# Summing V in four column tiles of the tensor engine, with per-pair sums on the vector engine, in a decode attention kernel

## The chip, the cores and the metric

One core of a Trainium2 chip. The metric is device time in microseconds (us) of one execution; lower is better. Engine names: PE is the tensor engine (PEld its weight loads), DVE the vector engine, ACT the scalar engine, POOL GpSimd, SP the engine that issues the input transfers.

## The reference

A gate mixes two branches; nearly all bytes and work are in branch A, a one-token attention over a cache.

```python
B, Sq, D = 4, 1, 1024
H, Sk, Dh = 32, 8192, 128          # k_cache, v_cache: (4, 32, 8192, 128) bf16 each
q = (x @ wq).reshape(B, Sq, H, Dh).transpose(0, 2, 1, 3)
scores = einsum("bhqd,bhkd->bhqk", q, k_cache) * Dh ** -0.5
p = softmax(scores)
o = einsum("bhqk,bhkd->bhqd", p, v_cache)
a = o.transpose(0, 2, 1, 3).reshape(B, Sq, H * Dh) @ wo
# branch B: a gated MLP, 1024 -> 3584 -> 1024, on the same four rows
# out = g * a + (1 - g) * b,  g = sigmoid(sum(x * gate_w))
```

K and V together are 537 MB, each read once. Everything else is 39 MB.

## The kernel before

The 128 heads are taken four at a time (a "pair" in the kernel's words is a K or a V load of four heads, 8 MB), 32 pairs of each. Four pairs form a group, which shares one softmax. SP loads into a ring of five 4 MB slots; a load waits until the slots are free. In the steady state the order is K pair d, then V pair d-4, and so on; the last four V pairs come alone, and then the output weights `wo`.

```python
# K pair (cut): DVE transposes a stretch, PE multiplies it
for n in range(RD):                                   # RD = 8 stretches
    flat_t = turned(P, CJ * P)                        # one of three transpose buffers
    nc.vector.transpose(out=flat_t.bitcast(U32), in_=kn[...])
    ... 8 matmuls 128x128 by 128x512 into S_ps ...

# V pair (cut): weights are the spread probabilities PB, 32 columns wide
row = NM * t                                          # NM = 32; t = pair in the group
for c in range(RD):
    for z in range(2):
        for w in range(2):
            for e in range(2):
                j0 = CJ * (c % JT) + 16 * z + 8 * w + 4 * e
                nc.tensor.matmul(o_ps[row:row + NM, e, :],
                                 lhsT=PB[:, RD * t + c, z, w]...,
                                 rhs=vn[:, j0 * Dh:(j0 + 4) * Dh],
                                 start=(n == 0), stop=(n == 4 * RD - 1))
if t < GD - 1:
    return
# once per group (cut): take from o_ps the half that is wanted, then select by matmul
nc.scalar.activation(out=o_sb[:], in_=o_ps[:, 0, :], func=ACT.Copy, scale=mE[:, 0:1])
nc.vector.scalar_tensor_tensor(out=o_sb[:], in0=o_ps[:, 1, :], scalar=mE[:, 1:2], in1=o_sb[:], ...)
... four fp32 matmuls with selg give oT ...

# output block (cut): eight matmuls with 4 rows, two column halves in turn
for r in range(r0, r1):
    for n in range(NH):
        mm_acc(acc[:, n * NB:(n + 1) * NB], LT[:, r, g, :], w[:, r, n * NB:(n + 1) * NB])
```

All 64 matmuls of one V pair write the same 32 rows of `o_ps`, that is, the same column tile of the array. At the end, behind the last V pair, the order on PE is: the last eight V matmuls, output block, selection, output block, a small turn of the new rows (`o_rows`), and 32 more output matmuls.

## Time and profile before

| | before |
|---|---|
| time | 1343.79 us median of 4 |
| bytes in | 576 MB at 429 GB/s |
| PE busy, DVE busy | 1032.8 us (77%), 614.4 us (46%) |
| one V pair on PE at full clock | 13.9 us |
| last V piece landed; last matmul ended | 1323.8 us; 1339.4 us |

These are lines of the page of the kernel before: busy time of each engine, then the span in 40 equal slices (busy tenths of PE; the granted clock of PE in tenths; the share of time in which the DMA engines were busy; what they moved).

```profile
PE 1032.8 (77%) x4552; PEld 227.9 (17%) x2364; DVE 614.4 (46%) x369; ACT 50.6 (4%) x46; POOL 62.8 (5%) x161
...
PE   2565878787788687778977779597778679877898
...
PEclk9787988888998888889988889888889899888899
DMA  9999999999999999999999999999999999999997
GB/s 414 436 432 431 439 434 427 445 430 422 445 424 430 442 432 426 438 434 428 438 436 426 432 430 434 436 433 438 428 423 436 430 431 442 436 419 444 419 425 325
```

The DMA row is full until the last slice. No engine is: the kernel is bound by the rate at which its bytes come in.

The costliest groups of instructions of the kernel before (line, engine, operation, output and inputs, shapes, count; then busy us and mean ns of one; then the idle time in front and what ended most of it). The view keeps different shapes apart.

```profile
L436 DVE STREAM_TRANSPOSE TB<-ring 128x2048 uint32<-128x2048 uint32 x256 | 566.9, 2277 | 492.4 <-DMA ring<-in_A_k_cache_dram 491.5 <-PE S_ps L442 0.8
L442 PE MATMUL S_ps<-TB,Z 128*128 128x512 bf16 x2048 | 518.8, 408 | 219.4 <-DVE TB L436 218.9
L513 PE MATMUL o_ps<-ring,PB 128*32 128x512 bf16 x2048 | 461.4, 388 | 52.6 <-DMA ring<-in_A_v_cache_dram 48.1 <-ACT PB L484 4.6
...
L457 DVE TENSOR_REDUCE mx<-S_ps 128x1 f32<-128x1024 f32 x8 | 9.8, 1225 | 15.9 <-PE S_ps L442 15.9
...
L307 PE MATMUL acc<-ring,xw 128*4 128x512 bf16 x56 | 3.7, 382 | 0.0
```

The mean of 388 ns is one matmul from start to end; they overlap, so the rate is the busy time over the count: 461.4 us / 2048 = 225 ns for V, but 3.7 us / 56 = 66 ns for the MLP's rows, which go to four column tiles in turn.

PE in the tail of the kernel before, in order of time (start us, duration us, what; in brackets the idle time in front and what ended it):

```profile
1323.80 1.89 PE L513 MATMUL o_ps<-ring,PB 128*32 128x512 bf16 x8 [0.61 <-DMA ring<-in_A_v_cache_dram]
1326.28 1.89 PE L273 MATMUL acc<-ring,LT 128*4 128x512 bf16 x8 [0.59 <-DMA ring<-in_A_wo_dram]
1328.10 1.06 PE L533 MATMUL small<-selg,OS 128*128 128x16 f32 x8
1329.09 1.89 PE L273 MATMUL acc<-ring,LT 128*4 128x512 bf16 x8
1330.82 0.33 PE L368 MATMUL small<-OT,identb 128*32 128x16 bf16 x16
1331.50 1.89 PE L273 MATMUL acc<-ring,LT 128*4 128x512 bf16 x8 [0.36 <-DVE LT L370]
1333.75 5.61 PE L273 MATMUL acc<-ring,LT 128*4 128x512 bf16 x24 [0.36 <-DMA ring<-in_A_wo_dram]
```

Here PE works nearly without a gap (busy for 12.25 us of the 13.9 us from 1326.1 us), at clock 1.00.

### The profile page before, as it was taken

What the parts mean: (1) busy time and instruction counts of PE and PEld (TensorE: products, weight loads), DVE (VectorE), ACT (ScalarE), POOL (GpSimd) and SP (SyncE); (2) the same over time, 40 slices, a digit from 0 to 9 for tenths busy, and PEclk for the clock granted to TensorE, in tenths of its full rate; (3) what the DMA queues carried; (4) which work ended last, traced back from release to release, by engine and by line L of the source; (5) the groups of instructions that cost most, each with busy time, mean ns of one, the idle gap of its engine ahead of it and who ended that gap; (6) DMA issues with size and microseconds to landing.
All of it is one profiled execution on the core that took longest, in us unless ns stands there. A gap on an engine that the chain in (4) does not pass through costs nothing.

```text
span 1342.2 us, 7696 instructions
## 1 busy us (share of the span) xinstructions
PE 1032.8 (77%) x4552; PEld 227.9 (17%) x2364; DVE 614.4 (46%) x369; ACT 50.6 (4%) x46; POOL 62.8 (5%) x161
## 2 busy tenths in 40 slices
PE   2565878787788687778977779597778679877898
PEld 0111111111111121111211112111111112111221
DVE  2555655545336554335455556046555254556000
ACT  0000100001000010001000010000100010000100
POOL 2000100001000010001000010000100010000100
PEclk9787988888998888889988889888889899888899
DMA  9999999999999999999999999999999999999997
GB/s 414 436 432 431 439 434 427 445 430 422 445 424 430 442 432 426 438 434 428 438 436 426 432 430 434 436 433 438 428 423 436 430 431 442 436 419 444 419 425 325
DMA packets 14316, 576.18 MB, mean 429 GB/s; under 512 B 1598, under 2 KB 1606, under 8 KB 2252
## 3 DMA queue, kind: packets, MB, share of 16 engines
q1 hardware_dynamic: 14276, 575.69, 99.5%
q8 instruction: 27, 0.44, 0.1%
q14 instruction: 5, 0.04, 0.0%
q10 hardware_dynamic: 8, 0.00, 0.0%
HBM read 575.68 MB, written 0.01 MB: 429 GB/s over the span
## 4 chain that ended last, share of the span: by engine, by line
DMA 66%; DVE 21%; PE 11%; another core or an unknown queue 1%; ACT 0%; issue 0%; SPq 0%; DVEq 0%
DMA ring<-in_A_k_cache_dram 58%; DVE TB L436 21%; PE o_ps L513 9%; DMA ring<-in_A_v_cache_dram 5%; DMA x<-in_gate_w_dram 2%; DMA ring<-in_A_wo_dram 1%; PE S_ps L442 1%; ACT PB L484 0%; PE S_ps L307 0%; PE acc L307 0%; PE acc L273 0%; PE small L533 0%; ACT OS L525 0%; PE small L472 0%
## 5 line engine op out<-in xcount | busy, mean ns | idle before, releaser
L436 DVE STREAM_TRANSPOSE TB<-ring 128x2048 uint32<-128x2048 uint32 x256 | 566.9, 2277 | 492.4 <-DMA ring<-in_A_k_cache_dram 491.5
L442 PE MATMUL S_ps<-TB,Z 128*128 128x512 bf16 x2048 | 518.8, 408 | 219.4 <-DVE TB L436 218.9
L513 PE MATMUL o_ps<-ring,PB 128*32 128x512 bf16 x2048 | 461.4, 388 | 52.6 <-DMA ring<-in_A_v_cache_dram 48.1
L442 PEld LDWEIGHTS <-Z 128*128 128x128 bf16 x1024 | 105.4, 103 | 628.0 <-issue 626.4
L513 PEld LDWEIGHTS <-PB 128*32 128x32 bf16 x1024 | 100.7, 98 | 405.1 <-issue 393.7
L421 POOL COPY Z<-qa 32x4 bf16<-32x4 bf16 x128 | 25.6, 200 | 761.6 <-PE S_ps L442 736.0
L486 POOL COPY PB<-PT 32x1024 bf16<-32x1024 bf16 x16 | 30.3, 1892 | 430.3 <-PE o_ps L513 426.2
L467 ACT ACTIVATE PTs<-S_ps,mx 128x1024 bf16<-128x1024 f32 x8 | 8.9, 1114 | 1020.9 <-DVE mx L463 1020.9
L526 DVE SCALAR_TENSOR_TENSOR OS<-o_ps,mE,OS 128x512 f32<-128x512 f32 x8 | 6.0, 751 | 72.2 <-ACT OS L525 72.2
L484 ACT COPY PB<-PT 32x1024 bf16<-32x1024 bf16 x16 | 30.5, 1908 | 1.5 <-DVE PT L469 1.3
L474 DVE RECIPROCAL rinv<-small 128x16 f32<-128x16 f32 x8 | 2.1, 258 | 42.0 <-PE small L472 42.0
L370 DVE CAST LT<-small 128x64 bf16<-128x64 f32 x2 | 0.4, 224 | 42.3 <-PE small L368 42.3
L236 PE MATMUL small<-identb,x 6*128 6x6 bf16 x8 | 0.6, 195 | 22.3 <-DMA x<-in_gate_w_dram 22.3
L457 DVE TENSOR_REDUCE mx<-S_ps 128x1 f32<-128x1024 f32 x8 | 9.8, 1225 | 15.9 <-PE S_ps L442 15.9
L273 PE MATMUL acc<-ring,LT 128*4 128x512 bf16 x64 | 14.8, 379 | 1.7 <-DMA ring<-in_A_wo_dram 1.0
L469 DVE STREAM_TRANSPOSE PT<-PTs 128x1024 bf16<-128x1024 bf16 x8 | 10.0, 1245 | 10.2 <-ACT PTs L467 10.2
L273 PE MATMUL acc<-ring,hT 128*4 128x512 bf16 x56 | 12.2, 379 | 0.0
L525 ACT ACTIVATE OS<-o_ps,mE 128x512 f32<-128x512 f32 x8 | 5.5, 687 | 162.8 <-PE o_ps L513 162.8
L307 PE MATMUL o_ps<-ring,xw 128*4 128x512 bf16 x56 | 5.7, 536 | 5.3 <-DMA ring<-in_B_w_gate_dram 5.3
L533 PEld LDWEIGHTS small<-selg,OS 128*128 128x128 f32 x64 | 9.0, 208 | 4.1 <-issue 3.9
L533 PE MATMUL small<-selg,OS 128*128 128x16 f32 x64 | 8.7, 269 | 0.0
L238 DVE COPY xw<-small 128x48 bf16<-128x48 bf16 x1 | 0.2, 181 | 15.9 <-PE small L236 15.9
(64 smaller groups left out, 67.2 us busy)
## 6 DMA issues: line engine op xcount, KB each, us to landing
ring<-in_A_k_cache_dram SPq DMA_DIRECT2D x14, 4096.0 KB, 34.1
ring<-in_A_v_cache_dram SPq DMA_DIRECT2D x14, 4096.0 KB, 31.4
ring<-in_B_w_gate_dram SPq DMA_DIRECT2D x1, 7168.0 KB, 37.1
ring<-in_B_w_up_dram SPq DMA_DIRECT2D x1, 7168.0 KB, 39.2
ring<-in_B_w_down_dram SPq DMA_DIRECT2D x2, 3584.0 KB, 27.4
ring<-in_A_wo_dram SPq DMA_DIRECT2D x6, 1024.0 KB, 24.7
ring<-in_A_v_cache_dram SPq DMA_DIRECT2D x2, 2048.0 KB, 28.7
ring<-in_A_v_cache_dram SPq DMA_DIRECT2D x4, 1024.0 KB, 24.7
```

Of the source, the lines that this page charges most:

```text
L273: nc.tensor.matmul(out_ap, lhsT=lhsT, rhs=rhs, start=start, stop=True, skip_group_check=True)
L421: nc.gpsimd.tensor_copy(out=Z[at, :, QP - 1 + QP * q], in_=qa[at, :, h0 + q, b])
L436: nc.vector.transpose(out=flat_t.bitcast(U32), in_=kn[:, c * CJ * Dh:(c + 1) * CJ * Dh].bitcast(U32))
L442: nc.tensor.matmul(sps[:, z, :], lhsT=Z[:, he, s:s + P], rhs=T[:, 16 * z:16 * z + 16, half, :, e], start=(t == 0 and n == 0 and he == 0), ...
L457: nc.vector.tensor_reduce(out=mx[:, 0:1], in_=sps[:].rearrange("p z n -> p (z n)"), axis=AX.X, op=ALU.max)
L467: nc.scalar.activation(out=PTs[:], in_=sps[:].rearrange("p z n -> p (z n)"), func=ACT.Exp, bias=negm[:, 0:1], scale=scale, accum_out=rs[:, ...
L469: nc.vector.transpose(out=PT[:].rearrange("p j i -> p (j i)"), in_=PTs[:])
L484: nc.scalar.copy(out=Bv[at, :, :, q, :], in_=Pv[at])
L486: nc.gpsimd.tensor_copy(out=Bv[at, :, :, q, :], in_=Pv[at])
L513: nc.tensor.matmul(o_ps[row:row + NM, e, :], lhsT=PB[:, RD * t + c, z, w].rearrange("p e s j -> p (e s j)"), rhs=vn[:, j0 * Dh:(j0 + 4) * ...
L526: nc.vector.scalar_tensor_tensor(out=o_sb[:], in0=o_ps[:, 1, :], scalar=mE[:, 1:2], in1=o_sb[:], op0=ALU.mult, op1=ALU.add)
L533: nc.tensor.matmul(oT[:, :], lhsT=o_sb[:, q * Dh:(q + 1) * Dh], rhs=selg[:, q].rearrange("p t s -> p (t s)"), start=(q == 0), stop=(q == 3))
```

## The change

The intent: PE spends 461 us on V, 225 ns per matmul, and every V matmul of a pair uses one column tile of 32 columns, while the MLP's rows, in four column tiles in turn, take 66 ns each. The change sends the four quarters of a stretch to four column tiles, so that their matmuls may overlap as those do. A pair then fills all 128 rows of `o_ps`, so it has to be summed before the next pair starts: a masked product and a row sum on DVE, per pair, in place of the selection once per group.

```diff
-    selg = const.tile([P, 4, GD, NQ], F32)
-    ...
-    mE = const.tile([P, 2], F32)
+    sel = const.tile([P, NQ], F32)
+    own = const.tile([P, 2, 4], F32)
     ...
-            if n == JT // 2 and d + 1 < ND:
-                spread(d + 1)
+            if n == 1:
+                flush_sums()
+                if d + 1 < ND:
+                    spread(d + 1)
     ...
+        flush_sums()
         for c in range(RD):
     ...
-                        nc.tensor.matmul(o_ps[row:row + NM, e, :],
+                        at = 32 * (2 * z + w)
+                        nc.tensor.matmul(o_ps[at:at + NM, e, :],
     ...
-                                 start=(n == 0), stop=(n == 4 * RD - 1),
+                                 start=(c == 0), stop=(c == RD - 1),
     ...
+        def sums():
+            kept = turned(P, 8 * Dh, F32)
+            nc.vector.tensor_tensor(out=kept.rearrange("p (k d) -> p k d", d=Dh), in0=o_ps[:]..., in1=own[:]..., op=ALU.mult)
+            nc.vector.tensor_reduce(out=o_own, in_=kept.rearrange("p (k d) -> p d k", d=Dh), axis=AX.X, op=ALU.add)
+        full.append(sums)
     ...
-        nc.scalar.activation(out=o_sb[:], in_=o_ps[:, 0, :], ...)
-        nc.vector.scalar_tensor_tensor(out=o_sb[:], in0=o_ps[:, 1, :], ...)
     ...
-                nc.tensor.matmul(oT[:, :], lhsT=o_sb[:, q * Dh:(q + 1) * Dh], rhs=selg[:, q]...)
+                nc.tensor.matmul(oT[:, i], lhsT=OS[:, i * Dh:(i + 1) * Dh], rhs=sel[:], ...)
     ... (the last sums are flushed ahead of the tail's output blocks)
```

More of the change, by code (lines that the diff above doesn't have):

```diff
@@ L248 @@
     mask = mask3[:].rearrange("p t q -> p (t q)")
-    selg = const.tile([P, 4, GD, NQ], F32)
-    one = ident[:].rearrange("p (t e s a) -> p e a t s", t=GD, e=2, s=NQ)
-    for a in range(4):
-        nc.vector.tensor_tensor(out=selg[:, a], in0=one[:, 0, a], in1=one[:, 1, a], op=ALU.add)
-    mE = const.tile([P, 2], F32)
-    nc.vector.tensor_reduce(out=mE[:], in_=id32[:].rearrange("p (e r) -> p e r", e=2), axis=AX.X, op=ALU.add)
+    sel = const.tile([P, NQ], F32)
+    nc.vector.tensor_reduce(out=sel[:], in_=id32[:].rearrange("p (e s j) -> p s e j", e=2, s=NQ), axis=AX.XY, op=ALU.add)
+    own = const.tile([P, 2, 4], F32)
+    nc.vector.tensor_reduce(out=own[:], in_=id32[:].rearrange("p (e s j) -> p e j s", e=2, s=NQ), axis=AX.X, op=ALU.add)
     mx, mxT, ng, ngT = [const.tile([P, 32], F32, name=f"mx{i}") for i in range(4)]
@@ L395, with flush_sums @@
     behind = []
+    full = []
+    def flush_sums():
+        while full:
+            full.pop(0)()
     def flush():
@@ L493, in v_pair @@
         g, t = divmod(d, GD)
-        row = NM * t
         if d == 0:
@@ L505, in v_pair @@
                     nc.sync.dma_start(out=vs[half][:, lo:hi], in_=vv[:, half * RING + lo:half * RING + hi])
-        n = 0
+        flush_sums()
         for c in range(RD):
@@ L512, in v_pair @@
                         j0 = CJ * (c % JT) + 16 * z + 8 * w + 4 * e
-                        nc.tensor.matmul(o_ps[row:row + NM, e, :],
+                        at = 32 * (2 * z + w)
+                        nc.tensor.matmul(o_ps[at:at + NM, e, :],
                                          lhsT=PB[:, RD * t + c, z, w].rearrange("p e s j -> p (e s j)"),
-                                         rhs=vn[:, j0 * Dh:(j0 + 4) * Dh], start=(n == 0), stop=(n == 4 * RD - 1),
+                                         rhs=vn[:, j0 * Dh:(j0 + 4) * Dh], start=(c == 0), stop=(c == RD - 1),
@@ L516, in v_pair @@
                                          skip_group_check=True)
-                    n += 1
-                    if n == 4:
-                        flush()
-                    if n == 16:
-                        flush_late()
+            if c == 0:
+                flush()
+            if c == 3:
+                flush_late()
+        o_own = OS[:, t * Dh:(t + 1) * Dh]
+        def sums():
+            kept = turned(P, 8 * Dh, F32)
+            nc.vector.tensor_tensor(out=kept.rearrange("p (k d) -> p k d", d=Dh), in0=o_ps[:].rearrange("p e (q d) -> p (e q) d", d=Dh),
+                                    in1=own[:].rearrange("p e q -> p (e q)").unsqueeze(2).to_broadcast([P, 8, Dh]), op=ALU.mult)
+            nc.vector.tensor_reduce(out=o_own, in_=kept.rearrange("p (k d) -> p d k", d=Dh), axis=AX.X, op=ALU.add)
@@ L522, in v_pair @@
+        full.append(sums)
         if t < GD - 1:
             return
-        o_sb = OS
-        nc.scalar.activation(out=o_sb[:], in_=o_ps[:, 0, :], func=ACT.Copy, scale=mE[:, 0:1])
-        nc.vector.scalar_tensor_tensor(out=o_sb[:], in0=o_ps[:, 1, :], scalar=mE[:, 1:2], in1=o_sb[:],
-                                       op0=ALU.mult, op1=ALU.add)
         flush_behind()
         def finish():
-            oT = small([P, GH])
-            for q in range(4):
-                nc.tensor.matmul(oT[:, :], lhsT=o_sb[:, q * Dh:(q + 1) * Dh],
-                                 rhs=selg[:, q].rearrange("p t s -> p (t s)"), start=(q == 0), stop=(q == 3))
+            oT = small([P, GD, NQ])
+            for i in range(GD):
+                nc.tensor.matmul(oT[:, i], lhsT=OS[:, i * Dh:(i + 1) * Dh], rhs=sel[:], start=True, stop=True,
+                                 skip_group_check=True)
@@ L536, in scaled @@
             def scaled():
                 hg = h0 + NQ - GH
-                nc.vector.scalar_tensor_tensor(out=OT[:, hg:hg + GH, b], in0=oT[:, :], scalar=sgb[:, 1, b:b + 1],
-                                               in1=rinv_t[g][:], op0=ALU.mult, op1=ALU.mult)
+                nc.vector.scalar_tensor_tensor(out=OT[:, hg:hg + GH, b], in0=oT[:].rearrange("p t s -> p (t s)"),
+                                               scalar=sgb[:, 1, b:b + 1], in1=rinv_t[g][:], op0=ALU.mult, op1=ALU.mult)
@@ L570 @@
     last += [wo_block(*cut) for cut in cuts]
+    flush_sums()
     last.pop(0)()
```

## The prediction

> **What bounds the kernel now: the input DMA.** The page counts 576.18 MB at a mean of 429 GB/s: 1343 us, the whole span (1342.2 us). In forty stretches of 33.5 us the DMA share is 0.97 to 1.04 everywhere but in the last, the tail (0.80). The chain of waits shows 29.7 to 41 us from a DMA's issue to its landing, while 8 MB at 429 GB/s need 19.5 us: at least 10 us of transfers are queued ahead at each issue, so the queue never starves. PE (1032.8 us, 77%) and DVE (614.4 us, 46%) have slack; a pair costs PE about 17.7 us for K and 13.9 us for V of some 39 us.
>
> **What the change does, costed.**
> - PE: the 2048 V matmuls and 1024 weight loads stay, but neighbours go to different column tiles and should overlap. The trace already has that pattern: the MLP's x rows (two matmuls per column tile, four tiles in turn) took 3.7 us for 56 (66 ns each) at full clock, 5.7 us for 56 (102 ns) at low clock, against 216 ns for V now. [...] Estimate: a V pair falls from 13.9 to 4.3-6.5 us, PE busy from 1033 to about 720 us (700 to 790).
> - DVE: per pair one fp32 masked product over 128x1024 from PSUM and one row sum of 1024. Same-sized operations in the trace: 1222 and 1225 ns. 32 x 2.45 = +78 us, less eight selections of 0.75 us: DVE about 687 us (51%). ACT loses 8 x 0.69 us.
> - Order: the sums sit behind the second transpose of the next K pair. The next V pair waits for them (one accumulator); only among the last four V pairs does this hold PE, about 2.6 us each.
>
> **How much is on the critical path: almost nothing.** K slots come free at most 2.5 us later, against 10 us queued ahead. V slots come free 5 to 9 us earlier, which only lengthens the queue. No byte is removed. I expect 427 to 431 GB/s as before.
>
> **Tail.** After the last V piece (1323.8 us) the selection took 0.69+0.75 us; now about 2.5 us, partly repaid by quicker matmuls and hidden behind an output block's eight matmuls, which end at 1328.1 us: 0 to 0.5 us lost. Also, PE was dense here (clock 1.00 in the last slices). With V three times quicker it idles between landings and may lose clock: in the trace, after 5 to 6 us idle the next 3 us run at 0.85 instead of 0.43 us per two matmuls. An output block would then take up to 3.4 instead of 1.9 us: 0 to 3 us lost.
>
> **Predicted: 1344.5 us, 1342.3 to 1347.5 in 8 of 10.** Faster by over 2%: 0.01; within 2%: 0.97; slower: 0.02.
>
> **What would show it.** PE busy near 720 us, V pairs near 5 us, DVE near 687 us, the two new groups near 1.22 us each; mean clock below 0.90; DMA share near 1.0 and 429 GB/s in every stretch; longer issue-to-landing of V and K; a lower clock in the last 20 us.
>
> **What would make it wrong.** Column tiles that do not overlap (PE stays near 1030 us; time still the same). Strided sums of 3 us or more, or DVE waiting for V long enough to empty the queue: DMA share below 0.95 mid-run. A DMA rate that depends on what PE and DVE do.

The 4.3 to 6.5 us for a V pair come from the trace's 66 and 102 ns, and 1344.5 us is the time before, 1343.79 us, and about 0.7 us for the tail.

## The result, and the profile after

1347.06 us median of 4 (1344.79 to 1348.08), against 1343.79 us. The ratio is 1.0022, with a 95% interval of 1.0007 to 1.0037. Ratios here are the mean time of one kernel's fast runs over that of the other's in the same rounds, so not quite the ratio of the medians quoted. It is a loss clear of noise, of 1.0 to 4.3 us, and the four runs spread over 3.3 us where those of before spread over 0.5 us.

The page of the changed kernel, the same lines:

```profile
PE 751.9 (56%) x4552; PEld 164.3 (12%) x2364; DVE 704.9 (52%) x422; ACT 45.8 (3%) x38; POOL 62.7 (5%) x161
...
PE   2665865544556654456565447356646355666346
...
PEclk9777987867788777779787778688778678888666
DMA  9999999999999999999999999999999999999997
GB/s 413 445 427 429 437 433 428 440 436 424 441 433 422 442 433 429 435 436 431 431 429 429 435 435 436 435 420 444 427 423 438 431 427 442 427 429 439 425 421 291
```

PE lost 281 us of busy time and DVE gained 90 us, and neither moved the span: the DMA row is as full as before. What did change is the clock row. It is lower almost everywhere, and its last three digits are 666 where they were 899.

Its groups that answer to those of before:

```profile
L446 PE MATMUL S_ps<-TB,Z 128*128 128x512 bf16 x2048 | 547.3, 418 | 463.8 <-DVE TB L440 463.8
...
L519 PE MATMUL o_ps<-ring,PB 128*32 128x512 bf16 x2048 | 143.8, 436 | 84.5 <-DMA ring<-in_A_v_cache_dram 84.5
...
L533 DVE TENSOR_REDUCE OS<-TB 128x128 f32<-128x1024 f32 x32 | 61.4, 1917 | 1.1
L531 DVE TENSOR_TENSOR TB<-o_ps,own 128x1024 f32<-128x1024 f32 x32 | 38.1, 1191 | 36.9 <-PE o_ps L519 36.9
```

V fell from 461.4 to 143.8 us, 70 ns per matmul on average. K rose from 518.8 to 547.3 us: the same matmuls, at a mean clock of 0.80 instead of 0.90. The row sum takes 1917 ns, the product 1191 ns.

PE in the tail of the changed kernel:

```profile
1323.68 1.05 PE L519 MATMUL o_ps<-ring,PB 128*32 128x512 bf16 x8 [1.43 <-DMA ring<-in_A_v_cache_dram]
1326.17 3.57 PE L272 MATMUL acc<-ring,LT 128*4 128x512 bf16 x8 [1.44 <-DMA ring<-in_A_wo_dram]
1329.67 1.87 PE L542 MATMUL small<-sel,OS 128*128 128x4 f32 x8
1331.47 3.57 PE L272 MATMUL acc<-ring,LT 128*4 128x512 bf16 x8
1334.84 0.33 PE L367 MATMUL small<-OT,identb 128*32 128x16 bf16 x16
1335.56 7.07 PE L272 MATMUL acc<-ring,LT 128*4 128x512 bf16 x32 [0.39 <-DVE LT L369]
```

Up to the last V piece nothing is lost: it lands at 1323.68 us, before at 1323.80 us, and the first output block's weights at 1326.17 us, before at 1326.28 us. Then the first output block takes 3.57 instead of 1.89 us (+1.68), the selection 1.87 instead of 1.06 us (+0.81), the second block +1.68. The final 32 matmuls take back 0.79 us (7.07 us instead of 7.86 us from 1331.50 to 1339.36, because they no longer wait for weights). With the 0.11 us of the earlier start: -0.11 + 1.68 + 0.81 + 1.68 - 0.79 = 3.27 us, and the last matmul ends at 1342.63 us instead of 1339.36 us. That is the whole difference between the two profiled runs (1347.21 and 1343.99 us).

The clock in stretches of about 3.4 us of the changed kernel (columns: stretch, its length, busy us and count of PE, PEld, DVE, ACT, POOL, then the granted clock, the DMA share and GB/s):

```profile
1318.10:1321.60 3.50, 1.46 (x14) 0.39 (x8) 0.00 (x0) 0.00 (x0) 0.00 (x0) 0.50 1.01 421
1321.60:1325.00 3.40, 1.69 (x16) 0.36 (x5) 0.22 (x1) 0.00 (x0) 0.00 (x0) 0.50 1.02 424
1325.00:1328.40 3.40, 2.23 (x6) 0.38 (x3) 2.89 (x2) 0.00 (x0) 0.00 (x0) 0.50 1.00 414
1328.40:1331.80 3.40, 3.40 (x13) 1.86 (x9) 0.22 (x1) 0.00 (x0) 0.00 (x0) 0.50 1.02 414
1331.80:1335.20 3.40, 3.37 (x24) 0.76 (x19) 0.03 (x1) 0.00 (x0) 0.00 (x0) 0.51 0.74 292
1335.20:1338.60 3.40, 3.04 (x15) 0.67 (x8) 0.22 (x1) 0.00 (x0) 0.00 (x0) 1.00 0.30 118
```

The clock is either 0.50 or 1.00. It fell at 1311.3 us and came back only at 1335.2 us. The changes at 1304.4, 1311.3 and 1335.2 us lie 6.83 and 23.89 us apart, two and seven times 3.413 us. The same holds for all the others: in the clock records of this trace (88) and of the trace of the kernel before (70) the changes lie whole multiples of 3.4133 us apart, to within 3 ns, and the shortest complete stretch at one clock is 3.413 us. Below, an interval is one such 3.413 us, ending where a change is or could be. What sets their length and their place the traces do not show.

### The profile page after: what moved, and what is told of

Read it like the earlier page. It is cut to its first block, busy times and chain, and to the rows that moved or that the text cites. A ratio compares the mean times of both kernels' runs of the same rounds, so it can differ in the third digit from the quotient of the medians.

```text
span 1345.4 us, 7748 instructions
## 1 busy us (share of the span) xinstructions
PE 751.9 (56%) x4552; PEld 164.3 (12%) x2364; DVE 704.9 (52%) x422; ACT 45.8 (3%) x38; POOL 62.7 (5%) x161
## 4 chain that ended last, share of the span: by engine, by line
DMA 68%; DVE 25%; PE 5%; another core or an unknown queue 1%; issue 0%; ACT 0%; DVEq 0%; SPq 0%
DMA ring<-in_A_k_cache_dram 59%; DVE TB L440 20%; DMA ring<-in_A_wo_dram 4%; DVE OS L533 3%; DMA ring<-in_A_v_cache_dram 3%; PE o_ps L519 2%; DVE TB L531 2%; DMA x<-in_A_x_dram 2%; PE S_ps L446 1%; PE acc L272 1%; PE S_ps L306 0%; PE small L542 0%; PE acc L306 0%; DVE mx L463 0%
## 5 line engine op out<-in xcount | busy, mean ns | idle before, releaser
L446 PE MATMUL S_ps<-TB,Z 128*128 128x512 bf16 x2048 | 547.3, 418 | 463.8 <-DVE TB L440 463.8
L519 PE MATMUL o_ps<-ring,PB 128*32 128x512 bf16 x2048 | 143.8, 436 | 84.5 <-DMA ring<-in_A_v_cache_dram 84.5
L533 DVE TENSOR_REDUCE OS<-TB 128x128 f32<-128x1024 f32 x32 | 61.4, 1917 | 1.1
L531 DVE TENSOR_TENSOR TB<-o_ps,own 128x1024 f32<-128x1024 f32 x32 | 38.1, 1191 | 36.9 <-PE o_ps L519 36.9
L519 PEld LDWEIGHTS <-PB 128*32 128x32 bf16 x1024 | 33.4, 107 | 186.3 <-issue 169.7
L272 PE MATMUL acc<-ring,LT 128*4 128x512 bf16 x64 | 18.5, 453 | 2.2 <-DMA ring<-in_A_wo_dram 1.4
L463 DVE TENSOR_REDUCE mx<-S_ps 128x1 f32<-128x1024 f32 x8 | 9.8, 1225 | 15.9 <-PE S_ps L446 15.9
L542 PEld LDWEIGHTS small<-sel,OS 128*128 128x128 f32 x64 | 9.8, 225 | 4.3 <-issue 4.2
L542 PE MATMUL small<-sel,OS 128*128 128x4 f32 x64 | 9.4, 271 | 0.0
## 6 DMA issues: line engine op xcount, KB each, us to landing
ring<-in_A_k_cache_dram SPq DMA_DIRECT2D x14, 4096.0 KB, 41.4
ring<-in_A_v_cache_dram SPq DMA_DIRECT2D x14, 4096.0 KB, 33.6
```

Of the source, the lines that this page charges most:

```text
L272: nc.tensor.matmul(out_ap, lhsT=lhsT, rhs=rhs, start=start, stop=True, skip_group_check=True)
L446: nc.tensor.matmul(sps[:, z, :], lhsT=Z[:, he, s:s + P], rhs=T[:, 16 * z:16 * z + 16, half, :, e], start=(t == 0 and n == 0 and he == 0), ...
L463: nc.vector.tensor_reduce(out=mx[:, 0:1], in_=sps[:].rearrange("p z n -> p (z n)"), axis=AX.X, op=ALU.max)
L519: nc.tensor.matmul(o_ps[at:at + NM, e, :], lhsT=PB[:, RD * t + c, z, w].rearrange("p e s j -> p (e s j)"), rhs=vn[:, j0 * Dh:(j0 + 4) * Dh ...
L531: nc.vector.tensor_tensor(out=kept.rearrange("p (k d) -> p k d", d=Dh), in0=o_ps[:].rearrange("p e (q d) -> p (e q) d", d=Dh), in1=own[:]. ...
L533: nc.vector.tensor_reduce(out=o_own, in_=kept.rearrange("p (k d) -> p d k", d=Dh), axis=AX.X, op=ALU.add)
```

## The experiments

Eleven kernels ran, one of them twice; the runs of the kernel before had medians of 1343.9 us, so times can be set side by side. The 95% interval of the ratio leaves out 1 only for the changed kernel, the column tiles alone and the kernel without the last sums; where smaller differences (0.4 to 0.9 us) are read below, they rest on five runs that lie above, or in one case almost above, all nine of the kernel before. Four kernels were wrong (named below). The comparison with the reference passed these too, so its tolerance does not see the part of the output that they spoil; it is no proof of the others, which are right by their construction.

The theory after reading the two traces: with V done four times as fast, PE idles between the last landings (1.43 us ahead of the last V piece), its clock falls to half (0.50), and the output blocks behind the last landing run at half speed on the critical path. The first rival: the sums on DVE, 3.1 us instead of 1.44 us behind the last V piece, hold up the tail. The second rival: the loss builds up over the whole run.

### The column tiles alone

The kernel before, with

```diff
-nc.tensor.matmul(o_ps[row:row + NM, e, :], ..., start=(n == 0), stop=(n == 4 * RD - 1),
+at = 32 * (2 * z + w)
+nc.tensor.matmul(o_ps[at:at + NM, e, :], ..., start=(c == 0), stop=(c == RD - 1),
```

> The kernel before with only its V matmuls moved to four column tiles; selection once per group as before; no sums on VectorE. Result wrong on purpose (each pair overwrites the last). Theory (the tensor engine idles between the last landings, loses its clock, and the output blocks after the last landing run slow): the loss stays, 1344.5 to 1348 us, PE busy about 750 us, DVE about 614 us, the two output blocks after the last V piece 3.4 to 3.6 us each, clock about 0.6 in the last 35 us. Rival (the sums on VectorE, 3.1 us instead of 1.44 us after the last V piece, make the loss): 1343.5 to 1344.1 us.

Measured: 1347.07 us median of 5, in two clusters (1344.42, 1344.63; 1347.07, 1347.23, 1347.30). PE busy 734.9 us, DVE 613.8 us, clock 0.64 in the last 33.5 us; the two output blocks took 3.57 and 3.33 us. The loss is there without any sum on DVE. The two quick executions have a mean clock of 0.784 and 0.785 over the whole run, the three others 0.777 to 0.781.

### The sums alone

The changed kernel, with

```diff
-at = 32 * (2 * z + w)
+at = 32 * t
-... start=(c == 0), stop=(c == RD - 1),
+... start=(c + z + w == 0), stop=(c == RD - 1 and z + w == 2),
-rhs=sel[:]
+rhs=selt[:, i]          # sel, cut to the 32 rows of pair i
```

> The changed kernel with its V matmuls back in one column tile per pair (row block t), the two sum operations per pair kept; the selection matrix is cut to the block, so the result is right. Theory of the clock: PE is dense again (busy about 1030 us, clock 1.00 in the last slices), DVE about 705 us, time 1343.6 to 1344.6 us, at most 0.8 us of loss from the longer sums. Rival of the sums: 1346 to 1348 us.

Measured: 1343.93 us median of 5, PE busy 1052.9 us, DVE 706.2 us, clock 1.00 in the last 67 us. So 92 us more of DVE work cost nothing in the median. But two of the five runs were at 1346.35 and 1346.62 us, with the same mean clock as the others (0.922), and no profile was taken of those. I come back to them.

### The tail held at full clock

The changed kernel, with useless matmuls between the pieces of the last V pair:

```diff
+            if d == ND - 1:
+                filler({1: 10, 3: 4}.get(c, 6 if c > 3 else 0))
+def filler(n):   # into the PSUM tile of the scores, which nobody reads any more
+    for _ in range(n):
+        nc.tensor.matmul(idle[0][:, 0, :], lhsT=identb[:], rhs=qa[:]..., start=True, stop=True)
```

> The changed kernel with 38 useless 128x512 matmuls put between the pieces of the last V pair, into a PSUM tile that nobody reads, so that PE has no gaps there. Result right. Theory of the clock: the output blocks after the last V piece take 1.9 us again, the last write is issued near 1340 us, time 1343.3 to 1344.3 us with a spread under 0.6 us. Rival of the sums, or of a DMA that lands later: 1346 to 1348 us as without them.

Measured: 1343.83 us median of 5, 1343.75 to 1344.21 us: the loss is gone, and the spread too. The timeline of PE in this kernel's tail:

```profile
1323.55 0.62 PE L526 MATMUL o_ps<-ring,PB 128*32 128x512 bf16 x8 [0.46 <-DMA ring<-in_A_v_cache_dram]
1324.11 1.47 PE L502 MATMUL S_ps<-qa,identb 128*128 128x512 bf16 x6
1326.04 1.89 PE L272 MATMUL acc<-ring,LT 128*4 128x512 bf16 x8 [0.47 <-DMA ring<-in_A_wo_dram]
1327.86 1.05 PE L551 MATMUL small<-sel,OS 128*128 128x4 f32 x8
1328.85 1.89 PE L272 MATMUL acc<-ring,LT 128*4 128x512 bf16 x8
```

The output blocks are at 1.89 us again and the selection at 1.05 us. The clock came back at 1312.6 us, while the first ten useless matmuls ran (1310.2 to 1313.7 us). Mean clock over the whole run is still only 0.819: what it is before the tail does not matter.

### The changed kernel without the very last sums

```diff
-        full.append(sums)
+        if d < ND - 1:
+            full.append(sums)
```

> The changed kernel without the two sum operations of the very last V pair (result wrong on purpose: a quarter of one group's rows is stale). Theory of the clock: the selection matmuls wait for the output block in front of them on PE, not for the sums, so nothing changes, 1344.5 to 1348 us. Rival of the sums: 1343.5 to 1344.5 us.

Measured: 1347.09 us median of 5 (1344.94 to 1348.46), the two blocks 3.57 us each. The sums are not what holds the tail: the selection waits behind the first output block on PE.

### Column tiles in the last four pairs only

The kernel before, tiled for the last four pairs (wrong, as the column tiles alone):

```diff
+tiled = d >= ND - GD
+at = 32 * (2 * z + w) if tiled else row
-nc.tensor.matmul(o_ps[row:row + NM, e, :], ..., start=(n == 0), stop=(n == 4 * RD - 1),
+nc.tensor.matmul(o_ps[at:at + NM, e, :], ..., start=(c == 0 if tiled else n == 0), stop=(c == RD - 1 if tiled else n == 4 * RD - 1),
```

> The kernel before, with column tiles for the V matmuls of the last four pairs only (result wrong on purpose for that group); all else as before, no sums. Theory of the clock in the tail: the whole loss comes back although 28 of 32 pairs are untouched: 1344.4 to 1347.5 us, output blocks after the last V piece 3.3 to 3.6 us, mean clock about 0.89. If the loss were built up over the whole run (slower K matmuls, later slots): 1343.6 to 1344.2 us.

Measured: 1344.84 us median of 5, all within 1344.71 to 1345.05 us; mean clock 0.884. The loss starts in the last four pairs, so it is not built up over the run; but it is about 0.9 us here and not 3 us. The timeline says why:

```profile
1326.12 3.57 PE L273 MATMUL acc<-ring,LT 128*4 128x512 bf16 x8 [1.43 <-DMA ring<-in_A_wo_dram]
1329.62 1.23 PE L535 MATMUL small<-selg,OS 128*128 128x16 f32 x8
1330.78 1.89 PE L273 MATMUL acc<-ring,LT 128*4 128x512 bf16 x8
```

Only the first block was slow. Here the clock came back at 1330.0 us, in the changed kernel's profile at 1335.2 us. The intervals start at another place: in this trace the one from 1326.6 to 1330.0 us lies wholly inside the first output block and the start of the selection (PE busy for all of it), and the clock is back at its end. In the changed kernel's profile the first block straddles the intervals 1325.0 to 1328.4 us (PE busy for 2.23 us) and 1328.4 to 1331.8 us; the second of these holds the end of the block and 1.87 us of small fp32 selection matmuls, PE counts as busy for all of it, and yet the clock stays at 0.50; it comes back only after the next interval, which the second output block fills. That the place of the intervals decides between the two clusters (about +0.5 to +1.1 us, and +3.1 to +4.5 us, over before) agrees with all five profiles of kernels with an idle tail and full-width blocks: clock back at 1329.1 and 1330.0 us in runs of 1344.44 and 1344.84 us, at 1334.5 to 1335.2 us in runs of 1347.00 to 1347.21 us.

A count over all fourteen traces supports this. The traces' clock records were cut into intervals of 3.413 us that end at the recorded changes. After 564 intervals at half clock the clock was full; each held at least 2.57 us of matmuls other than fp32. After 1085 it stayed at half; all but one held at most 2.61 us of them (the one, 2.72 us, is in the column tiles alone). Thirteen of these 1085 were busy throughout, but with fp32 matmuls for a good part, and held at most 2.37 us of others. In the traces of the kernels before and after alone it was full after 77, with at least 2.67 us, and stayed at half after 158, with at most 2.54 us; three of these were busy throughout, with 1.68 to 2.00 us of matmuls other than fp32. So in these traces the clock came back after intervals with about 2.6 us or more of matmuls other than fp32; this is a count, and no experiment varied that amount. In the changed kernel's tail only an interval that begins between 1325.4 and 1327.1 us holds that much of the first output block: 1.8 us of 3.4. The intervals lie at different places in the profiles of these five kernels: a change falls 0.55 us (changed kernel), 0.56 us (without the last sums), 1.33 us (the sum's terms side by side), 2.21 us (this kernel) and 3.29 us (column tiles alone) behind a whole multiple of 3.413 us from the span's start. If every place is equally likely, about half of the runs should be quick (an estimate from these figures), and of the twenty runs of these five kernels ten were: all five here, one of four of the changed kernel, two of five of the column tiles alone, one of five of the kernel without the last sums, and the single run of the sum's terms side by side (below). By the same estimate five quick runs out of five come about once in 25 times; whether that was luck I did not find out.

### One column tile again in the last four pairs

The changed kernel, with the V matmuls of the last four pairs in row block `t`, as in the sums-only kernel:

```diff
-at = 32 * (2 * z + w)
+apart = d < ND - GD
+at = 32 * (2 * z + w) if apart else 32 * t
-rhs=sel[:]
+rhs=sel[:] if d < ND - GD else selt[:, i]
 ... (start and stop as in the kernel that each pair follows)
```

> The changed kernel, with the V matmuls of the last four pairs back in one column tile each (result right). Theory of the clock: PE dense at the end, median 1343.6 to 1344.4 us, PE busy about 785 us; but the sums-only kernel had two of five runs at 1346.5 us with an unchanged mean clock, which the theory does not explain, and if that comes from the sums beside a dense PE in the last four pairs, one to three of these runs are there too. If the loss is built up over the run: 1346 to 1348 us.

Measured: 1343.94 us median of 5, four runs within 1343.80 to 1344.02 us, one at 1346.81 us; PE busy 771.9 us. So 28 of 32 pairs keep the column tiles at no cost; the loss is decided in the last four. The one slow run is of the kind of the sums-only kernel.

### The sum's terms side by side

```diff
-out=kept.rearrange("p (k d) -> p k d", d=Dh)      # product written in order
+out=kept.rearrange("p (d k) -> p k d", d=Dh)      # product written with a step of 8
-in_=kept.rearrange("p (k d) -> p d k", d=Dh)      # sum reads with a step of 128
+in_=kept.rearrange("p (d k) -> p d k", d=Dh)      # sum reads in order
```

> The changed kernel, with the masked product written so that the eight terms of one sum lie side by side; the row sum then reads its input in order, the product writes with a step of eight. The prediction took 1225 ns for the row sum from a reduction that reads in order; it measured 1917 ns. If the step of 128 elements (512 bytes) between the terms is the cause, the sum falls to 1.2 to 1.3 us, and the product stays at 1.2 us unless its strided write costs. If many outputs (128 of 8 terms instead of one of 1024) are the cause, it stays at 1.9 us. Time unchanged by either, 1344.5 to 1348 us.

Measured (one run, 1344.44 us), from its groups:

```profile
L531 DVE TENSOR_TENSOR TB<-o_ps,own 128x1024 f32<-128x1024 f32 x32 | 63.4, 1980 | 37.3 <-PE o_ps L519 37.3
L533 DVE TENSOR_REDUCE OS<-TB 128x128 f32<-128x1024 f32 x32 | 39.0, 1220 | 1.1
```

The sum fell to 1220 ns and the product rose from 1191 to 1980 ns. The number of outputs is not the cause; a step is, and it cost 0.7 to 0.8 us per 1024 elements here, both in what is read (512 bytes; 1917 against 1220 ns) and in what is written (32 bytes; 1980 against 1191 ns). No other step was tried, so what another one costs is not shown. Rearranging only moves the cost from one instruction to the other.

### The sums-only kernel once more

No edit.

> The sums-only kernel unchanged, once more, to catch one of its slow executions (two of five were at 1346.5 us) in a profile. If the clock in the tail is the cause, its last 30 us show stretches of clock 0.5; if late transfers are, its last V piece lands later than 1323.7 us; a fast one shows neither and is at 1343.6 to 1344.0 us.

Measured: 1343.93 us, a quick one; clock 1.00 throughout the tail. It tells nothing of the slow ones.

### Output halves in two column tiles

The changed kernel, with the two column halves of the output in rows 0 to 3 and 32 to 35, so that their matmuls can run side by side:

```diff
-acc = acc4[0:Bn].rearrange("p z n -> p (z n)")
+acc = [acc4[32 * n:32 * n + Bn, n, :] for n in range(2)]
-mm_acc(acc[:, n * NB:(n + 1) * NB], ...)
+mm_acc(acc[n], ...)
 ... (the last copies and writes take rows 0 to 3 and 32 to 35)
```

> The changed kernel, with the two column halves of the output accumulated in two column tiles (rows 0 to 3 and rows 32 to 35) instead of one after the other in one (result right). If the loss is the output blocks' PE time behind the last landings, an output block's eight matmuls fall to about 1.8 us at low clock and 0.9 us at full clock, PE waits for the last transfers again (last bytes near 1336.5 us), and the time is 1341.0 to 1343.0 us with a spread under 1 us, below both kernels. If the time hangs on anything else it stays at 1344.5 to 1348 us.

Measured: 1344.32 us median of 5, 1344.18 to 1344.58 us. The timeline of PE:

```profile
1326.48 1.87 PE L272 MATMUL acc<-ring,LT 128*4 128x512 bf16 x8 [1.44 <-DMA ring<-in_A_wo_dram]
1328.29 1.87 PE L542 MATMUL small<-sel,OS 128*128 128x4 f32 x8
1330.09 1.87 PE L272 MATMUL acc<-ring,LT 128*4 128x512 bf16 x8
...
1338.93 0.38 PE L272 MATMUL acc<-ring,LT 128*4 128x512 bf16 x2 [0.25 <-DMA ring<-in_A_wo_dram]
```

The clock was 0.50 until 1334.2 us, much as in the changed kernel (1335.2 us), and the blocks take 1.87 us all the same; most of the loss is gone and so are the two clusters. That is the same cause, met from the other side: not the clock as such, but PE's time behind the last landings. The hoped-for 1341 to 1343 us did not come. PE now waits for weights to the end: the last piece lands at 1338.9 us, not near 1336.5 us as I had read from the falling GB/s. So the kernel before, whose last matmul ended at 1339.4 us, was already within about half a microsecond of the last landing.

### The same in the kernel before

```diff
-mm_acc(acc[:, n * NB:(n + 1) * NB], ...)          # the edit of the experiment above,
+mm_acc(acc[n], ...)                               # in the kernel before
```

> The kernel before with the same two column tiles for the output and nothing else (result right). If the output blocks bound the tail at full clock too (32 matmuls in a row to the end), 1341.0 to 1343.0 us; if only the slow clock of the changed kernel made them matter, 1343.6 to 1344.0 us.

Measured: 1344.48 us median of 5, 0.6 us more than before, outside both expectations. PE again waits for the last piece (1338.86 us). My edit brought a cost of its own: the second half's output copy now waits for the first half's, as these lines of DVE's and then ACT's timeline show, so the last write is issued at 1340.60 instead of 1340.00 us. The changed kernel with output tiles pays it too (its last write is issued at 1340.67 us).

```profile
1339.28 0.68 DVE L579 CAST TB<-acc 4x512 bf16<-4x512 f32 x1 [9.06 <-PE acc L273]
```

```profile
1339.99 0.58 ACT L581 CAST TB<-acc 4x512 bf16<-4x512 f32 x1 [13.63 <-DVE TB L579]
```

### Both, with the clock held

The changed kernel with two edits, the output halves and the useless matmuls of the third experiment:

```diff
-mm_acc(acc[:, n * NB:(n + 1) * NB], ...)
+mm_acc(acc[n], ...)
+            if d == ND - 1:
+                filler({1: 10, 3: 4}.get(c, 6 if c > 3 else 0))
```

> The changed kernel with the two column tiles for the output and the 38 useless matmuls that hold the clock (result right). If the output tiles alone take PE off the path, the same as without the useless matmuls within 0.5 us; if the clock still counts, 0.5 to 1.5 us less.

Measured: 1344.40 us median of 5, equal to the changed kernel with output tiles (1344.32 us). With output tiles the clock no longer counts. No version beat the kernel before: the three tails with output tiles wait for the same landing of the last bytes (1338.7 to 1338.9 us) and all carry the copy's wait. A version without that wait was not tried.

### The sums alone, without the very last

The sums-only kernel with the edit of the fourth experiment (wrong):

```diff
-        full.append(sums)
+        if d < ND - 1:
+            full.append(sums)
```

> The sums-only kernel without the two sum operations of the very last V pair (result wrong on purpose). The sums-only kernel had two of six runs, and the changed kernel with a dense end one of five, at 1346.4 to 1346.8 us, all others at 1343.6 to 1344.0 us. If the longer sums after the last V piece leave PE so idle that in an unlucky phase its clock drops, all runs here are at 1343.5 to 1344.1 us. If the slow runs have another cause, about a third of them is at 1346.5 us again.

Measured: five runs of 1343.54 to 1343.95 us, none slow. With the last sums, three of eleven runs of the two kernels with a dense end were slow. If the last sums had nothing to do with it, five quick runs in a row would still come about one time in five ((8/11) to the fifth power, an estimate from these counts), so this only leans towards the last sums.

## Why the prediction was right or wrong

The prediction was right in its total and in its mechanism; its centre was 2.6 us low.

- **Bound by the input transfers: right.** The mean is 428 GB/s against 429, the DMA share is 0.97 to 1.03 in every stretch of 33.5 us but the last, and the last V piece lands 0.1 us earlier than before. PE is relieved of 281 us and DVE loaded with 90 us, and neither shows.
- **Column tiles overlap: right.** A V pair at full clock takes 3.61 us on the chain of waits where it took 13.93 us (3.9 times as long), a little better than the estimate of 4.3 to 6.5 us. PE was expected at 720 us (700 to 790) and came to 751.9 us; what the estimate left out is that K's own matmuls take 28.5 us more at the lower clock, a change seen beside the fall of the clock but not tested for itself.
- **DVE at 687 us: 18 us low (704.9 us).** The row sum was modelled on a reduction of the same size that reads in order (1225 ns); it reads with a step and takes 1917 ns. The experiment with the terms side by side shows that the step is the cause.
- **Slots and queue: right for V, in part for K.** V loads take 33.6 us from issue to landing instead of 31.4 us (24 others 33.4 instead of 31.3 us): more is queued ahead, as foretold. Of the K loads the 14 of 4 MB take 41.4 instead of 34.1 us, but the other 25 stay as they were (36.3 against 36.2 us). The hold of about 2.6 us foretold for each of the last V pairs does not show: the profile lists no V matmul that a sum released. One reading was wrong without effect: 17.7 us is what DVE's eight transposes take for a K pair; PE is busy for 518.8 / 32 = 16.2 us.
- **Tail, the sums (0 to 0.5 us): right.** Without the last sums the changed kernel is as slow.
- **Tail, the clock (0 to 3 us): the mechanism was right, and this is the term that was mis-sized.** The total allowed about 0.7 us for the whole tail. The profiled run lost 3.27 us: two output blocks at 1.68 us each and the selection at 0.81 us, less 0.9 us of waits that went and of an earlier start. I had doubled one block and had thought that a few microseconds of dense work would bring the clock back within it. When the clock came back went with the place of the 3.413 us intervals (by the five profiles and the count above; no experiment moved them), and in the changed kernel's profile, of the slow cluster, one interval was spent in part on small fp32 matmuls (1.87 us) and the clock stayed at 0.50. That the total came out inside the range is due to the width given to this term, and the centre would have been near for a quick run (1344.79 us). Five experiments show the cause: the column tiles alone bring the loss, the sums alone do not in the median, useless matmuls take it away, one column tile in the last four pairs takes it away but for one run in five, and output blocks that need half the PE time are spared most of it at the same low clock.

Open: what made three of eleven runs of the two kernels with sums and a dense end 2.4 to 2.9 us slower. No profile caught one. In the sums-only kernel the mean clock of the slow runs is not lower, which speaks against a long stretch of low clock; in the other the slow run has the lowest of five (0.824 against 0.825 to 0.827), too little to tell. Also open: what sets the place of the clock's intervals in a run.

## What to carry to other kernels

When the transfers are the bound, ask of any speed-up only what it does behind the last landing: there the change was worth minus 3 us, and everywhere else nothing. A tensor engine that is made faster in front of a critical tail may enter that tail with a lower clock, as here (0.50 instead of 1.00 at the first output block), so look at the clock row of the last slices and not only at busy time; the remedy can be to keep it busy, to leave its last work slow, or to make the tail itself need less of it. A duration borrowed from another instruction of the same size can fail when the access pattern differs (here 1917 instead of 1225 ns).
